# Forgetting attention and a GELU layer on one core: prefix sums on TensorE, w_in in smaller first pieces, an early first-layer product, v by SP's queue

## The chip, the cores and the metric

The kernel runs on one core of a Trainium2 chip. Its engines each follow their own instruction queue: TensorE (PE, with its weight loads PEld), VectorE (DVE), ScalarE (ACT), GpSimd (POOL) and SyncE (SP, which here only issues DMAs). The metric is the device time of one execution in microseconds; a kernel's time is the median of its runs. The time before is 332.49 us, the median of 3 runs (331.84 to 333.21).

## What is computed

Eight batches of eight heads, 576 positions, head size 64: causal attention in which each score gets the difference of two prefix sums of log f, followed by a two-layer MLP with a tanh GELU over the 4608 tokens (512 to 2048 to 512).

```python
scores = scale * np.matmul(q, k.transpose(0, 1, 3, 2))
log_f = np.log(np.clip(f, 0.0001, 1.0))
cum = np.cumsum(log_f, axis=-1)
decay = cum[:, :, :, None] - cum[:, :, None, :]
scores = np.where(causal, -1000000000.0, scores + decay)
attn = softmax(scores)                      # over the keys
x = np.matmul(attn, v)                      # heads side by side: 4608 x 512
h = x @ w_in
g = 0.5 * h * (1.0 + np.tanh(c * (h + 0.044715 * h * h * h)))
return g @ w_out
```

## The kernel before

**Quads.** Four heads of one batch are a quad; there are 16, two to a batch. A quad's queries and keys are loaded as bf16 (`LQ`, `LK`, by POOL's queue, which converts the type on the way) and transposed by DVE (`TQ`, `TK`, L209). The decay needs no work on the scores: the factor exp(-cum) of each key goes into the values (`vw`, on DVE, or `VW`, on POOL, L226) and into the weights of the denominators (`w_bf`); the query's factor cancels. So a quad is: scores on PE (`S`, or `H` for two of the four heads, L272), exp on ACT out of PSUM into `pt` (L280), causal masks on the diagonal blocks (`M` on POOL, L286; `m` as a multiply on DVE, L315), the denominators as a product on PE (`D`, followed on DVE by transpose, reciprocal, transpose), and two products with `vw` (`V`, x = 0 and 1) that DVE multiplies by the reciprocals into `xT` (L372). Quads 0 and 1, batch 0, are done in two parts of queries: part 0 is the first 256 positions, part 1 the other 320, and their scores come in four rounds, `split_rounds`. D.0.1 is quad 0, part 1; V.1.1.0 is quad 1, x = 1, part 0.

**The MLP.** Chunks of 512 tokens. Chunk 0's first layer is done in products of 256 tokens by 512 hidden columns: `J.half.g` (`mlp_in_half`, L404, 16 matmuls into a pair of PSUM banks of pool `psS`, then one GELU on ACT, L411). J.0.g needs part 0 of both quads in `xT`, J.1.g part 1. `F` and `f` are steps of the second layer (L597 for chunk 0, L530 later), f with 32-column weights; `I`, `E`, `U`, `UW`, `G`, `T` belong to the later chunks, whose products are saved by sums of blocks.

**The order is written out by hand.** `FRONT` is a string of words that are run one after the other; each engine gets its instructions in that order, and each queue its DMAs. A word `A@B` adds a wait: the first DMA of A starts only when B's has landed. `B.n.cols` issues n products of zeros of that many columns into `idle_ps`, a tile in the pool `psO` (one buffer, which `D` and `V` of the later quads use), so that PE has something to do. `X` and `Y` load ACT's table for exp and GELU.

**The prefix sums** (`SB` and `CW`). f is clipped by DVE, its logarithm taken by ACT, transposed on PE (L630) and copied to `logfT`, 5 tiles of 128 positions by 64 heads. POOL adds up the tiles before each tile (`before`, L648 and L650), and PE makes cum as a product with a triangle (L656, 320 columns) plus a product of ones with `before` (L657, 256 columns). ACT's exp of it is `wT`.

**Loads in the front.** POOL's queue has k and q of quads 0 and 1, then v of batch 0 row by row of 128 positions (`LP.t`), w_in in four pieces of 1024 hidden columns by half of the model dimension (`WI.c`, 8 KB of fp32 a partition), w_out in four (`WO.c`), v of batch 1 (`LX`: half of the heads, five DMAs), and the next quads' k and q. `Z` is five memsets on POOL. SP's queue carries f, and later v and the output. `LU.t` and `LV` are the same loads as `LP` and `LX` on SP's queue.

Of the kernel before, what the change touches and what calls it, by code (L numbers as in the profile page):

```python
# [8 lines left out]
FP32 = mybir.dt.float32  # L9
# [7 lines left out]
def kernel(  # L17
# [20 lines left out]
    D_MODEL, D_FF = moe_w_in.shape  # L38
# [20 lines left out]
    QA = 256  # L59
# [26 lines left out]

    SECOND = """
# [21 lines left out]
    singles = ctx.enter_context(tc.tile_pool(name="singles", bufs=1))  # L109
# [21 lines left out]
    vw = many(2, [128, NT + 1, 4, D], BF16, "vw")  # L131
# [4 lines left out]
    gT = singles.tile([128, N_FT, CH], BF16, name="gT")  # L136
# [13 lines left out]
    spare = singles.tile([1, 1], FP32, name="spare")  # L150
# [224 lines left out]
    def mlp_in(c, pr):  # L375

        n0 = CH * c % RING
        spans = [(n0, CH)] if n0 + CH <= RING else [(n0, HC), ((n0 + HC) % RING, HC)]
        ph = psS.tile([128, 2, 512], FP32, name="ps_h", tag="s")
        for dts in (range(N_DT - 1), range(N_DT - 1, N_DT)):  # L380
            for j in range(2):
                ft = 2 * pr + j
                for dt in dts:
                    for n, (h0, cols) in enumerate(spans):
                        nc.tensor.matmul(  # L385
                            ph[:, j, n * cols:(n + 1) * cols],
                            w_in_sb[:, dt, 128 * ft:128 * ft + 128],
                            xT[:, dt, h0:h0 + cols],
                            start=(dt == 0 and n == 0), stop=(dt == N_DT - 1),
                            skip_group_check=True,  # L390
                        )
                    if dt == N_DT - 1 and j == 1:
                        nc.scalar.activation(gelus(c, 2 * pr, 2), ph, AF.Gelu_apprx_tanh)  # L393
                    yield

    def mlp_in_half(half, g):

        ph = psS.tile([128, 2, 512], FP32, name="ps_h", tag="s")
        n0 = QA * half
        for dts in (range(N_DT - 1), range(N_DT - 1, N_DT)):  # L400
            for j in range(4):
                ft = 4 * g + j
                for dt in dts:
                    nc.tensor.matmul(  # L404
                        ph[:, j // 2, QA * (j % 2):QA * (j % 2) + QA],
                        w_in_sb[:, dt, 128 * ft:128 * ft + 128],
                        xT[:, dt, n0:n0 + QA],
                        start=(dt == 0 and j % 2 == 0), stop=(dt == N_DT - 1),
                        skip_group_check=True,
                    )  # L410
        nc.scalar.activation(gT[:, 4 * g:4 * g + 4, n0:n0 + QA],  # L411
                             ph.rearrange("p a (b n) -> p (a b) n", n=QA), AF.Gelu_apprx_tanh)

    def x_block(c, b, t):
        n0 = (CH * c + HC * t) % RING
        return xT[:, 2 * b:2 * b + 2, n0:n0 + HC]
# [227 lines left out]
            copy(m, utri_f32)  # L644
        copy(causal[1][64:128, 0:64], utri_f32[0:64, 0:64])

    def sums_before(eng):
        eng.tensor_copy(before[:, 0:BH], logfT[:, 0:BH])  # L648
        for t in range(1, NT - 1):
            eng.tensor_add(before[:, t * BH:(t + 1) * BH],  # L650
                                 before[:, (t - 1) * BH:t * BH],
                                 logfT[:, t * BH:(t + 1) * BH])

    def make_w():
        cum_ps = psM.tile([128, NT * BH], FP32, name="cum_ps", tag="m")
        nc.tensor.matmul(cum_ps, utri_f32, logfT, start=True, stop=False)  # L656
        nc.tensor.matmul(cum_ps[:, BH:], ones_f32, before, start=False, stop=True)  # L657
# [15 lines left out]
    def unit_part(c, u, n, spare=False):  # L673
        pull(units.setdefault((c, u), unit(c, u, spare)), n)
# [11 lines left out]
    def load_values(b, half):  # L686
# [104 lines left out]
```

## Time and profile before

| | us |
|---|---|
| median of 3 runs | 332.49 |
| the profiled execution | 332.24 |
| its span, first to last instruction | 330.4 |
| PE busy | 318.3 (96%) |
| DVE busy | 227.8 (69%) |
| ACT busy | 203.4 (62%) |
| POOL busy | 111.2 (34%) |

A busy PE counts idle products too, and a matmul at half clock as busy. The mean granted clock over the span is 0.990. Landmarks of the front, in us from the span's start: k and q of quad 0 land at 5.4 and 6.9; the cumulative sums end at 10.05; the first scores of quad 0 run at 10.69; the exps of quads 0 and 1 run from 11.49; D.0.1 ends at 26.05; the last product of chunk 0's first layer ends at 46.08; the second layer follows directly.

In a timeline row the first number is the start, the second the time to the end of the merged group, then engine, line, operation, output and input tiles, and the count; in square brackets stands the idle time before it and what ended it. In a row of waits: who waited for whom, total us, times, longest.

### The profile page before, as it was taken

The page shows a single profiled execution, that of the slowest core. Times are in us where ns is not written, and L with a number is a line of the kernel's source. Part 1 is how long each engine was busy: PE and PEld are TensorE (multiplying, and loading weights), DVE is VectorE, ACT ScalarE, POOL GpSimd, SP SyncE. Part 2 cuts the span into 40 slices and gives each one's busy share as a digit, 9 for nine tenths or more (in the row PEclk, how much of TensorE's full clock was granted, in tenths as well). Part 3 has the DMA queues.
Part 4 walks back from the last instruction along what each step waited for, and adds up shares of the span by engine and source line. Part 5 has one row for each costly group of instructions (what it writes and reads, how often), then busy time and mean ns, then how long its engine had stood idle before and what let it go on. Part 6 is the DMA issues. An engine that isn't in the chain of part 4 may idle for free.

```text
span 330.4 us, 12071 instructions
## 1 busy us (share of the span) xinstructions
PE 318.3 (96%) x5474; PEld 215.4 (65%) x5474; DVE 227.8 (69%) x360; ACT 203.4 (62%) x242; POOL 111.2 (34%) x155
## 2 busy tenths in 40 slices
PE   3988999999999999999999999999999999999996
PEld 1345864554677567765878877657765776587585
DVE  5574416985999967697777786779665865465373
ACT  4584476686766685587648765776668743712810
POOL 8985654152032506431444134412550140000000
PEclk9996999999999999999999999999999999999999
DMA  7999799576051991197118911661020102012002
GB/s 129 219 199 209 109 194 225 137 137 147 2 107 44 245 190 52 38 202 133 52 38 181 155 54 36 152 115 50 8 96 0 34 6 97 0 34 95 2 32 95
DMA packets 44322, 33.42 MB, mean 101 GB/s; under 512 B 27488, under 2 KB 37856, under 8 KB 44272
## 3 DMA queue, kind: packets, MB, share of 16 engines
q0 software_dynamic: 8848, 16.58, 28.2%
q1 hardware_dynamic: 35280, 16.01, 18.5%
q8 instruction: 42, 0.69, 0.8%
q10 hardware_dynamic: 144, 0.07, 0.1%
q14 instruction: 8, 0.07, 0.1%
HBM read 36.85 MB, written 9.44 MB: 140 GB/s over the span
## 4 chain that ended last, share of the span: by engine, by line
PE 92%; POOL 3%; DVE 2%; issue 1%; ACT 1%; POOLq 0%; DVEq 0%
PE ps_w L530 29%; PE ps_h L385 26%; PE ps_s L272 9%; PE po L340 9%; PE ps_u L451 6%; PE ps_h L404 5%; PE pso L597 4%; PE po_m L326 2%; PE idle_ps L251 1%; DVE pt L315 1%; ACT pt L280 1%; POOL v_nat L180 1%; POOL vw L226 1%; PE ps_o L340 0%; POOL q_c L203 0%
## 5 line engine op out<-in xcount | busy, mean ns | idle before, releaser
L280 ACT ACTIVATE pt<-ps_s 128x1024 bf16<-128x1024 f32 (+2 forms) x100 | 93.8, 988 | 48.0 <-PE ps_s L272 45.3
L385 PE MATMUL ps_h<-xT,w_in_sb 128*128 128x512 bf16 (+1 forms) x448 | 92.4, 356 | 0.0
L286 POOL TENSOR_SCALAR_AFFINE_SELECT pt<-pt 128x512 bf16<-128x512 bf16 (+3 forms) x65 | 39.6, 619 | 118.7 <-ACT pt L280 117.9
L385 PEld LDWEIGHTS <-w_in_sb 128*128 128x128 bf16 x448 | 43.8, 98 | 36.2 <-issue 0.4
L393 ACT ACTIVATE gT<-ps_h 128x1024 bf16<-128x1024 f32 x44 | 44.7, 1017 | 22.6 <-PE ps_h L385 22.2
L530 PEld LDWEIGHTS <-gT 128*32 128x32 bf16 (+1 forms) x1354 | 45.0, 97 | 3.8 <-issue 0.4
L530 PE MATMUL ps_w<-w_out_sb,gT 128*32 128x256 bf16 (+1 forms) x954 | 41.3, 273 | 0.0
L530 PEld LDWEIGHTS <-gsum 128*32 128x32 bf16 (+1 forms) x984 | 35.3, 97 | 3.4 <-issue 1.5
L272 PE MATMUL ps_s<-qT,kT 32*128 32x64 bf16 (+5 forms) x896 | 37.1, 266 | 0.1
L226 POOL TENSOR_TENSOR vw<-v_nat,wT 128x1280 bf16<-128x1280 f32 (+1 forms) x13 | 29.5, 2267 | 10.4 <-DMA v_nat<-in_v_dram 6.9
L209 DVE STREAM_TRANSPOSE kT<-k_c 128x576 f32<-128x576 f32 x16 | 19.9, 1246 | 12.2 <-DMA k_c<-in_k_dram 12.2
L272 PEld LDWEIGHTS <-kT 32*128 32x128 bf16 x896 | 17.1, 93 | 17.1 <-issue 12.0
L530 PE MATMUL ps_w<-usum,gsum 128*32 128x256 bf16 (+1 forms) x779 | 28.3, 273 | 0.0
L547 DVE COPY snap<-ps_w 128x512 f32<-128x512 f32 x32 | 21.6, 676 | 7.8 <-PE ps_w L530 7.8
L372 DVE TENSOR_TENSOR xT<-po,rb 128x576 bf16<-128x576 f32 x26 | 19.6, 756 | 9.9 <-PE po L340 9.2
L340 PE MATMUL po<-pt,vw 128*32 128x64 bf16 (+4 forms) x624 | 22.5, 279 | 0.0
L508 DVE TENSOR_TENSOR gsum<-gT 128x1024 bf16<-128x1024 bf16 x14 | 9.7, 692 | 18.3 <-ACT gT L464 13.1
L467 DVE TENSOR_TENSOR usnap<-ps_u,usnap 128x512 f32<-128x512 f32 x21 | 13.8, 683 | 12.3 <-PE ps_u L451 7.9
L340 PEld LDWEIGHTS <-vw 128*32 128x32 bf16 x672 | 14.4, 97 | 10.5 <-issue 3.7
L209 DVE STREAM_TRANSPOSE qT<-q_c 128x576 f32<-128x576 f32 x16 | 19.9, 1243 | 1.3 <-PE ps_s L272 0.7
L464 ACT ACTIVATE gT<-usnap 128x512 bf16<-128x512 f32 x18 | 11.1, 630 | 9.5 <-DVE usnap L467 9.5
L530 PE MATMUL ps_w<-w_out_sb,gsum 128*128 128x256 bf16 (+2 forms) x205 | 16.6, 269 | 0.0
(109 smaller groups left out, 414.5 us busy)
## 6 DMA issues: line engine op xcount, KB each, us to landing
out_dram<-o_st SPq DMA_DIRECT2D x35, 256.0 KB, 2.3
k_c<-in_k_dram POOLq DMA_DIRECT2D x16, 288.0 KB, 5.7
q_c<-in_q_dram POOLq DMA_DIRECT2D x16, 288.0 KB, 6.2
v_nat<-in_v_dram SPq DMA_DIRECT2D x16, 256.0 KB, 4.7
w_in_sb<-in_moe_w_in_dram POOLq DMA_DIRECT2D x4, 512.0 KB, 9.7
w_out_sb<-in_moe_w_out_dram POOLq DMA_DIRECT2D x4, 512.0 KB, 7.1
v_nat<-in_v_dram SPq DMA_DIRECT2D x16, 128.0 KB, 3.8
v_nat<-in_v_dram POOLq DMA_DIRECT2D x13, 128.0 KB, 7.5
```

The costliest lines, as they stand in the source:

```text
L209: nc.vector.transpose(out=dst.rearrange("p s c -> p (s c)").bitcast(FP32) .rearrange("p (t a) -> p a t", a=S // 32), in_=src.rearrange("p ...
L226: eng.tensor_mul(vw[i % 2][:, t0:t1], vb[:, t0:t1, h0:h0 + 4, :], wT[:, i, t0:t1, :].unsqueeze(3).to_broadcast([128, t1 - t0, 4, D]))
L272: nc.tensor.matmul(tiles[h // 2][:, h % 2, c0:c0 + nq], key_columns(i, key, h, c), qq[32 * h:32 * h + 32, q0:q0 + nq, c], start=(c == 0 an ...
L280: nc.scalar.activation(p[:, 2 * g:2 * g + 2, off:off + n], t[:, :, 0:n], AF.Exp, scale=scale)
L286: nc.gpsimd.affine_select(out=x, in_=x, compare_op=ALU.is_ge, fill=0.0, base=0, pattern=pattern, channel_multiplier=-1)
L340: nc.tensor.matmul(po[r0:r0 + w.shape[-1], 448 + q0:448 + q0 + nq], w, p[:, h, col:col + nq], start=(key in (0, "low")), stop=(key in ("lo ...
L372: nc.vector.tensor_mul(xT[:, 2 * u + x, r0 + s0:r0 + s1], po, rbs[i, part])
L385: nc.tensor.matmul(ph[:, j, n * cols:(n + 1) * cols], w_in_sb[:, dt, 128 * ft:128 * ft + 128], xT[:, dt, h0:h0 + cols], start=(dt == 0 and ...
L393: nc.scalar.activation(gelus(c, 2 * pr, 2), ph, AF.Gelu_apprx_tanh)
L451: nc.tensor.matmul(ps[:, n, :], w[:, d, 128 * n:128 * n + 128], x[:, d, :], start=(first and n == 0 and d == 0), stop=(d == 1), skip_group ...
L530: nc.tensor.matmul(ps[c0:c0 + width, n, cols[0]:cols[1]], x[:, j, 128 * n + c0:128 * n + c0 + width], w[:, j, cols[0]:cols[1]], start=(fir ...
L547: copy(kept[name], ps)
```

## The change

The prefix sums move from POOL to PE; w_in's first 1024 hidden columns come in pieces of 512; one product of the first layer, J.0.0, is made early as `j.0.0` in the bank pair that the idle products used, and its GELU is issued later, as `GJ.0.0`; part of batch 0's v and the halves of later batches that POOL's queue brought go by SP's queue; and the words of `FRONT` stand in a new order. No `B` follows `j.0.0` any more. After the cut the rest of the order up to the end of `FRONT` holds the same work with small moves (F.1's steps are 97 in both).

```diff
     SETUP = """
-        TK.0 LP.4 LP.0 LP.1
+        TK.0 LP.0 LP.1
     """
     FRONT = """
-        TQ.0 SB TR B.1.512 TK.1 LP.2@LQ.0 CW B.1.256 B.1.512 WI.0 S.0.0 B.5.384 TQ.1 S.0.2 LQ.2 B.2.512 Z H.1.0.1 vw.0.0 B.2.128 vw.1.0 M.0.0 LP.3
-        B.1.128 WI.1@LU.4 H.1.1.1 B.3.384 W WI.3 WI.2 H.1.0.0 M.1.0.1 D.0.0 M.1.0.0 H.0.1.1 V.0.0.0 H.0.1.0 B.3.128 H.1.1.0 M.0.1 V.0.1.0 D.1.0 H.0.3.0
-        vw.0.1 LX.1.1 V.1.0.0 H.0.3.1 m.0.3.2 V.1.1.0 H.1.3.0 B.1.256 m.0.3.4 VW.1.1 H.1.3.1 D.0.1 M.1.3 S.1.2 M.1.1 V.0.0.1 LK.2 V.0.1.1 WO.0 J.0.1
-        D.1.1 WO.1@LV.1.1 J.0.0 V.1.1.1 V.1.0.1 VW.3 J.0.3 J.1.3 WO.2@WI.1 J.1.1 WO.3 J.1.0 LK.3 LQ.3 TQ.2 J.0.2 LQ.4 TK.2 LX.1.0@WO.2 J.1.2 X B.1.128
-        f.0.6 LK.4 TK.3 S.2.0 LK.5 f.0.5 F.0.4 S.2.2 F.0.10 S.2.1 TQ.3 TQ.4 F.0.10 m.2.1 LV.2.0@LK.5 vw.2 S.3.0 TK.4 CL.2 M.2.2 f.0.7 LQ.5 M.2.0 D.2
+        Z CW TR TQ.0 B.1.512 WI.1 WI.0 LU.3@LU.1 S.0.0 B.5.384 LU.2@LU.0 TQ.1 TK.1 S.0.2 LU.4@LU.1 B.2.512 H.1.0.1 vw.0.0 M.0.0 vw.1.0 B.2.128 B.1.384
+        WI.3 WI.2 B.1.256 H.1.1.1 B.1.256 W H.1.0.0 M.1.0.1 B.1.512 LQ.2 D.0.0 M.1.0.0 H.0.1.1 WI.4 V.0.0.0 B.2.128 H.0.1.0 M.0.1 V.0.1.0 LV.1.1@WI.3
+        H.1.1.0 WI.5 D.1.0 H.0.3.0 B.2.128 V.1.0.0 H.0.3.1 m.0.3.2 V.1.1.0 H.1.3.0 vw.0.1 j.0.0 H.1.3.1 m.0.3.4 M.1.3 D.0.1 S.1.2 M.1.1 VW.1.1 V.0.0.1
+        LK.2 V.0.1.1 WO.0 GJ.0.0 D.1.1 V.1.1.1 J.0.1 WO.1@LV.1.1 V.1.0.1 J.1.1 WO.2 J.0.2 TQ.2 WO.3 J.1.0 J.0.3 TK.2 LQ.3 LK.3 VW.3 J.1.2 LQ.4 J.1.3
+        LV.1.0@WO.2 X F.0.1 LK.4 TK.3 F.0.4 F.0.1 S.2.0 f.0.8 f.0.3 S.2.2 F.0.10 S.2.1 TQ.3 TQ.4 LK.5 F.0.10 LV.2.0@LK.5 m.2.1 S.3.0 vw.2 CL.2 M.2.2
...
     def load_w_in(c):
-        n, u = D_FF // 2, c % 2
-        s = slice(n * (c // 2), n * (c // 2 + 1))
+        u, n = c % 2, D_FF // 4
+        s = (slice(0, n), slice(n, 2 * n), slice(2 * n, 4 * n))[c // 2]
...
+    later = {}
+
-    def mlp_in_half(half, g):
+    def mlp_in_half(half, g, spare=False):
 
-        ph = psS.tile([128, 2, 512], FP32, name="ps_h", tag="s")
+        if spare:
+            ph = psO.tile([128, 1024], FP32, name="ps_h", tag="po").rearrange("p (a n) -> p a n", n=512)
+        else:
+            ph = psS.tile([128, 2, 512], FP32, name="ps_h", tag="s")
...
-        nc.scalar.activation(gT[:, 4 * g:4 * g + 4, n0:n0 + QA],
+        later[half, g] = lambda: nc.scalar.activation(gT[:, 4 * g:4 * g + 4, n0:n0 + QA],
                              ph.rearrange("p a (b n) -> p (a b) n", n=QA), AF.Gelu_apprx_tanh)
+        if not spare:
+            later[half, g]()
...
-    def sums_before(eng):
-        eng.tensor_copy(before[:, 0:BH], logfT[:, 0:BH])
-        for t in range(1, NT - 1):
-            eng.tensor_add(before[:, t * BH:(t + 1) * BH],
-                                 before[:, (t - 1) * BH:t * BH],
-                                 logfT[:, t * BH:(t + 1) * BH])
-
     def make_w():
         cum_ps = psM.tile([128, NT * BH], FP32, name="cum_ps", tag="m")
-        nc.tensor.matmul(cum_ps, utri_f32, logfT, start=True, stop=False)
-        nc.tensor.matmul(cum_ps[:, BH:], ones_f32, before, start=False, stop=True)
+        nc.tensor.matmul(cum_ps, utri_f32, logfT, start=True, stop=True)
+        for n in range(NT - 1, 0, -1):
+            nc.tensor.matmul(cum_ps[:, n * BH:], ones_f32, logfT[:, :(NT - n) * BH], start=False, stop=True,
+                             skip_group_check=True)
...
+        "j": lambda half, g: mlp_in_half(half, g, True),
+        "GJ": lambda half, g: later[half, g](),
```

At the end of `FRONT` the load of batch 3's second half of v, `LX.3.1@LK.6`, becomes `LV.3.1@LK.6`.

More of the change, by code (lines that the diff above doesn't have):

```diff
@@ L79 @@
-        D.1.1 WO.1@LV.1.1 J.0.0 V.1.1.1 V.1.0.1 VW.3 J.0.3 J.1.3 WO.2@WI.1 J.1.1 WO.3 J.1.0 LK.3 LQ.3 TQ.2 J.0.2 LQ.4 TK.2 LX.1.0@WO.2 J.1.2 X B.1.128
-        f.0.6 LK.4 TK.3 S.2.0 LK.5 f.0.5 F.0.4 S.2.2 F.0.10 S.2.1 TQ.3 TQ.4 F.0.10 m.2.1 LV.2.0@LK.5 vw.2 S.3.0 TK.4 CL.2 M.2.2 f.0.7 LQ.5 M.2.0 D.2
-        S.3.1 f.0.7 m.3.0 V.2.0 S.3.2 f.0.6 TK.5 f.0.1 M.3.2 CL.3 V.2.1 S.4.1 m.3.1 LQ.6 F.0.6 TQ.5 H.4.2.1 D.3 LQ.7 H.4.0.1 VW.4 H.4.0.0 V.3.1 v.3.0
-        f.0.2 H.4.2.0 LV.2.1@LQ.5 LK.6 I.1.1 U.0 m.4.1 I.1.4 I.1.6 I.1.0 TQ.6 U.1 m.4.2.3 I.1.5 m.4.2.2 CL.4 LV.3.0@LQ.7 M.4.0 TK.6 G.0 I.1.2 U.3 I.1.3
@@ L83 @@
-        U.2 I.1.7 G.1.1.2 X UW.2.1 UW.2.2 F.1.20 UW.2.3 VW.5 S.5.0 F.1.19 S.5.1 D.4 M.5.0 f.1.12 S.5.2 V.4.0 f.1.9 m.5.2.3 V.4.1 CL.5 m.5.2.2 LQ.8
-        UW.2.4 S.6.0 M.5.1 f.1.12 D.5 S.6.1 f.1.7 LK.7 V.5.1 f.1.7 vw.6 S.6.2 V.5.0 f.1.11 m.6.1 M.6.2.2 m.6.0 m.6.2.3 LK.8 CL.6 LX.3.1@LK.6
+        Z CW TR TQ.0 B.1.512 WI.1 WI.0 LU.3@LU.1 S.0.0 B.5.384 LU.2@LU.0 TQ.1 TK.1 S.0.2 LU.4@LU.1 B.2.512 H.1.0.1 vw.0.0 M.0.0 vw.1.0 B.2.128 B.1.384
+        WI.3 WI.2 B.1.256 H.1.1.1 B.1.256 W H.1.0.0 M.1.0.1 B.1.512 LQ.2 D.0.0 M.1.0.0 H.0.1.1 WI.4 V.0.0.0 B.2.128 H.0.1.0 M.0.1 V.0.1.0 LV.1.1@WI.3
@@ new lines @@
+        H.1.1.0 WI.5 D.1.0 H.0.3.0 B.2.128 V.1.0.0 H.0.3.1 m.0.3.2 V.1.1.0 H.1.3.0 vw.0.1 j.0.0 H.1.3.1 m.0.3.4 M.1.3 D.0.1 S.1.2 M.1.1 VW.1.1 V.0.0.1
+        LK.2 V.0.1.1 WO.0 GJ.0.0 D.1.1 V.1.1.1 J.0.1 WO.1@LV.1.1 V.1.0.1 J.1.1 WO.2 J.0.2 TQ.2 WO.3 J.1.0 J.0.3 TK.2 LQ.3 LK.3 VW.3 J.1.2 LQ.4 J.1.3
+        LV.1.0@WO.2 X F.0.1 LK.4 TK.3 F.0.4 F.0.1 S.2.0 f.0.8 f.0.3 S.2.2 F.0.10 S.2.1 TQ.3 TQ.4 LK.5 F.0.10 LV.2.0@LK.5 m.2.1 S.3.0 vw.2 CL.2 M.2.2
+        f.0.7 M.2.0 D.2 S.3.1 LQ.5 f.0.6 V.2.0 m.3.0 TK.4 S.3.2 f.0.1 CL.3 LK.6 TK.5 f.0.3 f.0.2 M.3.2 V.2.1 S.4.1 m.3.1 LQ.6 F.0.6 TQ.5 H.4.2.1 D.3
@@ L85 @@
+        H.4.0.1 H.4.0.0 VW.4 V.3.1 v.3.0 f.0.2 H.4.2.0 I.1.1 LV.2.1@LQ.5 LQ.7 U.0 m.4.1 I.1.4 I.1.6 TQ.6 m.4.2.3 I.1.0 I.1.5 m.4.2.2 CL.4 LV.3.0@LQ.7
+        U.1 TK.6 M.4.0 G.0 U.2 I.1.2 UW.2.1 U.3 I.1.3 I.1.7 G.1.1.2 F.1.20 UW.2.2 X S.5.0 UW.2.3 VW.5 F.1.19 S.5.1 D.4 M.5.0 f.1.12 S.5.2 V.4.0 f.1.10
+        UW.2.4 m.5.2.3 m.5.2.2 V.4.1 CL.5 LQ.8 M.5.1 S.6.0 f.1.13 D.5 S.6.1 f.1.5 V.5.1 f.1.9 LK.7 vw.6 S.6.2 V.5.0 m.6.1 M.6.2.2 m.6.0 F.1.2
+        LV.3.1@LK.6 m.6.2.3 F.1.7 CL.6 LK.8
     """
@@ L144 @@
     logfT = singles.tile([128, NT * BH], FP32, name="logfT")
-    before = singles.tile([128, (NT - 1) * BH], FP32, name="before")
     wT = singles.tile([128, NQ, NT, 4], FP32, name="wT")
@@ L692 @@
         "CW": make_w,
-        "SB": lambda: sums_before(nc.gpsimd),
-        "sb": lambda: sums_before(nc.vector),
         "Z": zeros,
```

## The prediction

> **What bounds the kernel now.** I read the slices of the span first, then the waits of PE, then the first 47 us window by window, then each engine's timeline there. In the page's slices PE is full but for the first and for one dent, and in the fourth slice (24.8 to 33.0 us) the granted clock falls to 0.6.
>
> ```profile
> PE   3988999999999999999999999999999999999996
> PEclk9996999999999999999999999999999999999999
> ```
>
> So PE bounds everything, and time can only come from the front. What PE waited for up to 80 us, and the windows of 1 us around the dent (sum, then PE, PEld, DVE, ACT, POOL busy, then clock, DMA share, GB/s):
>
> ```profile
> PE po_m L326 <- DVE pt L315: 2.3, 2, 1.5
> PE cum_ps L657 <- POOL before L650: 1.1, 1, 1.1
> ```
>
> ```profile
> 22.00:23.00 1.00, 0.98 (x19) 0.58 (x18) 1.00 (x3) 1.00 (x3) 1.00 (x3) 1.00 1.04 182
> 23.00:24.00 1.00, 0.24 (x12) 0.07 (x7) 1.00 (x2) 0.66 (x1) 1.00 (x2) 1.00 1.17 213
> 24.00:25.00 1.00, 0.31 (x8) 0.10 (x8) 1.00 (x2) 0.00 (x0) 1.00 (x2) 0.67 1.08 203
> 25.00:26.00 1.00, 0.17 (x8) 0.10 (x8) 0.78 (x1) 0.00 (x0) 1.00 (x2) 0.50 1.11 215
> 31.00:32.00 1.00, 1.00 (x15) 0.65 (x17) 0.00 (x0) 0.11 (x1) 0.59 (x1) 0.92 1.20 192
> ```
>
> The denominators of quad 0's second part (D.0.1) wait for two masks on DVE (m.0.3.2, m.0.3.4); behind them PE is idle for most of 22.8 to 26.05 us, and the clock is at half from 24.34 us (0.67 in that window) to 31.16 us (0.92). That costs twice: the stage after the wait is slow too, as the chain of waits shows, where 16 matmuls of the first layer take 3.00 us and later 96 take 10.59 us, 1.77 for 16:
>
> ```profile
> 28.85 3.00 PE ps_h L404 x16
> ...
> 35.49 10.59 PE ps_h L404 x96
> ```
>
> Of the slow 6.82 us PE worked in 26.05 to 31.16, so half of 5.11, 2.55 us, is lost to the clock. Why the masks are late stands in the timelines of DVE and POOL: the first takes 1.36 us while POOL issues five loads of v, the second 1.65 us while POOL makes vw; the same mask with POOL idle takes 0.42 us (56.23).
>
> ```profile
> 20.47 3.65 POOL L180 DMA_DIRECT2D v_nat<-in_v_dram  x5
> 24.11 1.51 POOL L226 TENSOR_TENSOR vw<-v_nat,wT 128x768 bf16<-128x768 f32 x1
> ...
> 22.51 1.36 DVE L315 TENSOR_TENSOR pt<-pt,causal 128x512 bf16<-128x512 bf16 x1
> 24.13 1.65 DVE L315 TENSOR_TENSOR pt<-pt,causal 128x256 bf16<-128x256 bf16 x1
> 56.23 0.42 DVE L315 TENSOR_TENSOR pt<-pt,causal 128x512 bf16<-128x512 bf16 x1
> ```
>
> Ahead of it, from 11.5 to 23.7 us, ACT's exps run almost without a gap (pitch 0.65, 0.73 and 0.9 us for 640, 768 and 1024 columns), and each score product on PE waits for the exp two before it.
>
> **The change, step by step.** I follow PE through the new order; "before" is the same event in the trace.
>
> Prefix sums. POOL's copy and three additions (7.26 to 8.79) go, and PE's wait of 1.07 us. In place of one 256-column product there are four, 64 to 256 columns, 640 in all. The trace has two such shapes:
>
> ```profile
> 6.35 1.41 PE L656 MATMUL cum_ps<-logfT,utri_f 128*128 128x320 f32 x2
> ...
> 8.83 1.22 PE L657 MATMUL cum_ps<-before,ones_f 128*128 128x256 f32 x2 [1.07 <-POOL before L650]
> ```
>
> The difference of 0.19 us for 64 columns, 3.0 ns a column, is the low bound: 1.9 us; with each product's fixed 0.45 us (1.22 less 256 x 3.0 ns) it is 3.7 us. I take 2.9, the middle, since weight loads (0.25 us each) overlap partly. From 7.7 that ends at 10.6 (9.6 to 11.4), before 10.05. Of the idle products behind it 256 columns are gone (0.64 us before, about 0.3 now), so S.0.0 starts at 10.95 instead of 10.69 and its exps at 11.8 instead of 11.49.
>
> DVE's new order (causal copies ahead of TQ.0, TQ.1 ahead of TK.1): qT is ready at 8.8, before S.0.0; kT of quad 1 is ready at 13.96 (q lands at 11.44, two transposes of 1.26), before 11.16, and H.1.0.1 starts only at 14.9, when an exp frees its bank. Cost nothing; without that cover it would be 2.8.
>
> Exps and idle products up to H.1.3.0. S.0.2's exps start at 14.15 (13.85). H.1.0.1 is now followed by 128, 128, 384 and 256 idle columns (0.58 us by rows of 0.09, 0.20 and 0.20) instead of three of 128 (0.27), and 256 and 512 columns stand where 3 x 384 (0.59) stood; another 256 follow V.0.0.0 and 256 D.1.0. With scores of 0.5 to 0.6 and products of 0.3 us PE is now as long as ACT's pitch: H.1.1.1's exp starts at 16.7 (16.00), H.0.1.1's at 18.6 (17.87), H.0.3.1's at 22.4 (21.40), H.1.3.0 ends on PE at 23.15 (22.02). So the front arrives 1.1 us later here (0.3 to 1.9 by the bounds above).
>
> The early product j.0.0, 16 matmuls, 1.77 us, goes here, 23.15 to 24.95. It needs w_in's first 512 columns, issued at about 8.1 and 8.8 behind POOL's memsets (1.7 us, moved up); the 1024-column piece issued at 9.62 landed 7.8 us later, so they are there by 17 to 18. It needs xT from V.1.1.0 for its last four: with the loads of v off POOL's queue the mask m.0.3.2 starts with its exp at 23.15 and takes 0.42, then V.1.1.0's multiply 0.41, to 24.0; the last four start at 24.5. Then vw.0.1 (0.92, moved behind) to 24.9 and m.0.3.4, 0.27, to 25.2. SP now brings v's rows 2, 3 and 4, issued when rows 0 and 1 have landed (14.35 before); SP's loads of v took 4.2 us, so they are there by 20. Only other loads of v stand behind that wait in SP's queue. H.1.3.1 runs 24.95 to 25.5 and its exp ends at 26.25 (23.67). D.0.1 starts at 25.5 with its masks done, so the wait of 2.3 us is gone and PE has no gap from which the clock would fall.
>
> One rule speaks against the mask's 0.42 us. The Trainium skill, SBUF — State Buffer, "Who interferes with whom", has a vector instruction with two SBUF inputs block against a GpSimd instruction that reads SBUF, and infers that it does not against the writing of DMA descriptors. The 1.65 us beside vw agrees (it ends 0.16 us behind it); the 1.36 us beside mere DMA issues does not. By the rule m.0.3.2 would stay at 1.36 and the sum below come out 0.6 us smaller.
>
> What is late next. POOL had made vw for V.1.1.1 by 25.6; now it masks first: 1.70 us for M.1.3 and M.1.1, then 1.51 for VW.1.1, all behind H.1.3.1's exp, to 29.5. PE meanwhile: D.0.1 to 26.15, S.1.2 to 26.65 (its second bank is free at 26.3), V.0.0.1 and V.0.1.1 1.15, D.1.1 from 28.0 (S.1.2's exps) to 28.65; then V.1.1.1 waits 0.9 to 29.55. V.1.1.1 0.58, J.0.1 1.77, V.1.0.1 0.58, two matmuls of J.1.1, then a wait of 0.4 for V.1.0.1's multiply (0.49), since nothing stands between: J.1.1 ends at 34.65. The remaining five J at 1.77 end at 43.5. GJ.0.0 and the table load (1.28 and 1.02) lie on ACT at 28 to 30.5, under these products. Before, the last J ends at 46.08 and 0.06 of idle product follows: **2.6 us** earlier.
>
> The loads. Q of quad 2 is issued behind half of w_in, k behind VW.1.1 at 29.5 (27.2); w_out's four go at 30.1 to 32.4, before 27.8, 31.4, 37.9 and 38.7 (landed 45.5), since they no longer stand behind VW.3. By 1888 KB of such loads landed in 12.5 us from 37.93, 151 KB a us, quad 2's k and w_out, 2336 KB, need 15.5 us: 45.0, or 47.9 if quad 3's q and k and v's half (another 1152 KB) interleave, at the 190 KB a us of those windows. F.0's twelfth step, which first needs the last piece, comes at 47.1 (six steps of 0.235, S.2.0 0.7, six more). I take nothing; up to 0.8 if not.
>
> Behind 46 us PE is full in every window up to 262, the work is the same, and order and queues (v by SP for batches 1 and 3, k and q some places later) only move cover. I take nothing, with 0.5 either way.
>
> **Sum.** 330.4 - 2.6 = 327.8 of span; the execution was 332.24 and the median 332.49, so 329.6 for that execution and 329.9 for the median.
>
> **Rivals.**
> (1) The masks stay slow beside POOL: 2.0 us gained, 330.5. For it the rule above; against it that POOL issues nothing between WI.5 (about 21) and M.1.3 (26.3).
> (2) Loads are late: w_out (0.8) and with it quad 3's transposes take back 1.6 us: 331.5. For it the DMA share of 1.0 from 2 to 37 us; against it the pause at 38 to 40 (0.01), which goes, and SP's cheaper bytes (8.9% of the engines for 1.88 MB against 80.9% for 10.97).
> (3) The front's shift eats the gain: the prefix sums take 3.7 us, 0.8 more, and the idle products and the scores behind them slip by as much again: j.0.0 starts at 24.75 and 1.0 remains: 331.5. For it the exps' pitch, which leaves PE no slack from 16 us on; against it that ACT waits too, so that a slip before 16 us is partly made good.
> (4) Slower: the wait moves to V.1.1.1 and takes the clock along. POOL's 3.2 us chain hangs on H.1.3.1's exp, which j.0.0 pushes back 2.6. The clock fell about 1.4 us after PE's steady work ended (22.95 to 24.34), so from a wait of 1.4 instead of 0.9 it falls again, and the work of the next seven us runs at half: 0.5 + 3.3 lost, 333.7. For it: nothing in that chain is spare, each of POOL's four instructions there follows on the one before. Against it: PE works right up to that wait. The Trainium skill, TensorE: Matmul & The Clock Gate, Part 1, has the clock decided in free-running windows of about 3.4 us; by that a wait of 1.4 alone would not do it, though before the 3.2 us of idling here fit.
>
> **Numbers.** Forecast 0.58, (1) 0.10, (2) 0.10, (3) 0.10, (4) 0.12. Half a per cent (1.66 us) is about what a measurement of this kernel tells from no change: faster is below 330.83, the forecast but for a tenth and most of (1), some of the rest: 0.65; slower, above 334.15, only the worse half of (4) and the unforeseen: 0.09; the rest 0.26. The forecast's own range is 328.3 to 331.2 (prefix sums and idle products 0.8, tail 0.5); with (2) and (3), each with 1.3 for the same unknowns, it reaches 332.8, and (4) with 0.12 is left out.
>
> **What would show it.** Right: granted clock 1.0 from 10 to 46 us; L315's masks under 0.5 us; j.0.0 without a gap, ending near 25; the last J near 43.5; a new wait of about 0.9 on POOL's vw. Wrong: a second dent in the clock near 29 to 36, waits on w_in or w_out, or cumulative sums ending past 11.4.

## The result and the profile after

The changed kernel took 328.17 us in the median of 20 runs (326.76 to 334.38), the kernel before beside it 332.26 (330.57 to 333.71). The ratio is 0.9867, with a 95% interval of 0.9848 to 0.9887: faster by about 4.4 us, where 2.6 were forecast. Thirteen of the 20 executions lie between 326.8 and 329.0; seven took 331.9 to 334.4, and the comparison leaves those out. They have a cause of their own, shown below: the profile that was taken of the changed kernel is one of them (334.38), so the usual execution is read from a second profile of the very same kernel (run a_again, 327.39, span 325.7 against 330.4 before).

The slices of its page, PE's busy share and the granted clock:

```profile
PE   3998999999999999999999999999999999999996
PEclk9999999999999999999999999999999999999999
```

The dent of the fourth slice is gone, in PE as in the clock. What PE waited for up to 80 us, behind the prefix sums, and three of the windows round the old dent (sum, then PE, PEld, DVE, ACT, POOL busy, then clock, DMA share, GB/s):

```profile
PE po_m L326 <- POOL vw L226: 0.4, 1, 0.4
PE ps_s L272 <- ACT pt L280: 0.4, 1, 0.4
PE ps_h L409 <- DVE xT L372: 0.3, 1, 0.3
```

```profile
22.00:23.00 1.00, 1.00 (x12) 0.87 (x9) 1.00 (x3) 0.32 (x1) 0.00 (x0) 1.00 1.15 201
...
24.00:25.00 1.00, 0.98 (x28) 0.33 (x20) 0.59 (x2) 0.58 (x2) 0.39 (x1) 1.00 1.04 144
25.00:26.00 1.00, 1.00 (x40) 0.82 (x41) 0.86 (x3) 1.00 (x2) 1.00 (x3) 1.00 1.03 158
```

The wait of 2.3 us is gone and with it the seven us at half clock. What is left are three waits of 0.3 to 0.4, for vw at 27.7 us, for an exp in S.0.2 at 12.5 and for xT at 31.2, and the clock stays at 1.00. PE's timeline has j.0.0, H.1.3.1 and D.0.1 without a wait, and DVE's the two masks:

```profile
21.32 1.92 PE L409 MATMUL ps_h<-xT,w_in_sb 128*128 128x256 bf16 x16
23.17 0.52 PE L272 MATMUL ps_s<-qT,kT 32*128 32x320 bf16 x8
23.62 0.70 PE L326 MATMUL po_m<-pt,w_bf 128*32 128x320 bf16 x20
```

```profile
21.61 0.42 DVE L315 TENSOR_TENSOR pt<-pt,causal 128x512 bf16<-128x512 bf16 x1 [0.59 <-ACT pt L280]
...
23.15 0.28 DVE L315 TENSOR_TENSOR pt<-pt,causal 128x256 bf16<-128x256 bf16 x1
```

So far this is what was forecast. The rest of the gain, nearly 2 us, appears in PE's timeline of the first microseconds. First the kernel before, then a_again:

```profile
10.63 0.82 PE L272 MATMUL ps_s<-qT,kT 32*128 32x256 bf16 x16
11.38 1.78 PE L251 MATMUL idle_ps<-idle 128*128 128x384 bf16 x5
13.10 0.72 PE L272 MATMUL ps_s<-qT,kT 32*128 32x320 bf16 x8
```

```profile
7.48 2.55 PE L658 MATMUL cum_ps<-logfT,ones_f 128*128 128x64 f32 x8
9.83 0.63 PE L251 MATMUL idle_ps<-idle 128*128 128x512 bf16 x1
10.40 0.52 PE L272 MATMUL ps_s<-qT,kT 32*128 32x256 bf16 x16
10.85 0.99 PE L251 MATMUL idle_ps<-idle 128*128 128x384 bf16 x5
11.81 0.32 PE L272 MATMUL ps_s<-qT,kT 32*128 32x320 bf16 x2
```

The same five idle products take 1.78 us before and 0.99 after, the same 16 score products 0.82 and 0.52. The array was at about half speed there in the kernel before, though the page's clock row has 9 in those slices and the windows 1.00. The clock record in the trace explains it: its first entry, full speed, stands at 14.10 us in the kernel before and at 10.36 in a_again, and the page counts the time ahead of the first entry as full speed. S.0.2's first scores run at 11.81 instead of 13.10.

| event, us | before | forecast | a_again |
|---|---|---|---|
| S.0.0 starts | 10.69 | 10.95 | 10.46 |
| S.0.2's exps start | 13.85 | 14.15 | 12.89 |
| H.1.1.1's exp starts | 16.00 | 16.7 | 15.25 |
| H.1.3.0 ends on PE | 22.02 | 23.15 | 21.38 |
| j.0.0 ends | | 24.95 | 23.24 |
| D.0.1 ends | 26.05 | 26.15 | 24.32 |
| wait of V.1.1.1 for vw | | 0.9 | 0.40 |
| last J ends | 46.08 | 43.5 | 41.65 |

The last J ends 4.4 us earlier, and the execution is 4.85 shorter than the profiled one before: nothing of it is given back behind the last J.

**The long executions.** In the first profile of the changed kernel the front is as in a_again up to 28 us. Then POOL's timeline has, and PE's waits answer it:

```profile
28.34 0.76 POOL L196 DMA_DIRECT2D w_out_sb<-in_moe_w_out_dram  x1
38.23 2.23 POOL L196 DMA_DIRECT2D w_out_sb<-in_moe_w_out_dram  x3 [9.13 <-DMA v_nat<-in_v_dram]
```

```profile
PE pso L604 <- DMA w_out_sb<-in_moe_w_out_dram: 5.3, 3, 3.0
```

`WO.1@LV.1.1` holds POOL until SP has brought the second part of v for batch 1. Those five loads of SP took 9.6 to 14.7 us to land, with a median of 11.5, and SP was held up in issuing them too, as the chain of waits shows (start, us, what):

```profile
22.25 5.76 SPq L180
28.06 9.64 DMA v_nat<-in_v_dram
```

So the last three loads of w_out go out at 38.23. From 35 to 39 us the DMA engines are nearly idle (share 0.07 in that window): POOL waits, and nothing else has been issued. The second layer's first products (L604) then wait for w_out, three times, and the clock is at 0.50 from 52 to 55 us. In a_again POOL's wait for v is 3.14 us, the loads go out at 32.12, and PE does not wait for w_out up to 80 us. Why SP's loads land later in some executions than in others, no run here shows.

```profile
32.12 2.23 POOL L196 DMA_DIRECT2D w_out_sb<-in_moe_w_out_dram  x3 [3.14 <-DMA v_nat<-in_v_dram]
```

### The profile page after: what moved, and what is told of

It is laid out like the page before. It is cut to its first block, busy times and chain, and to the rows that moved or that the text cites. A ratio compares the mean times of both kernels' runs of the same rounds, so it can differ in the third digit from the quotient of the medians.

```text
span 332.7 us, 11990 instructions
## 1 busy us (share of the span) xinstructions
PE 315.8 (95%) x5426; PEld 215.8 (65%) x5444; DVE 225.6 (68%) x360; ACT 203.6 (61%) x242; POOL 97.7 (29%) x135
## 4 chain that ended last, share of the span: by engine, by line
PE 82%; DMA 8%; POOL 3%; SPq 2%; issue 2%; DVE 1%; ACT 1%; POOLq 0%; DVEq 0%
PE ps_w L537 28%; PE ps_h L385 26%; PE po L340 8%; PE ps_s L272 8%; PE ps_u L458 6%; PE pso L604 4%; DMA w_out_sb<-in_moe_w_out_dram 3%; DMA v_nat<-in_v_dram 3%; SPq L180 2%; DMA w_in_sb<-in_moe_w_in_dram 2%; ACT pt L280 1%; POOL pt L286 1%; PE cum_ps L658 1%; POOL vw L226 1%; DVE vw L226 0%
## 5 line engine op out<-in xcount | busy, mean ns | idle before, releaser
L604 PE MATMUL pso<-w_out_sb,gT 128*32 128x512 bf16 (+1 forms) x157 | 16.4, 388 | 5.8 <-DMA w_out_sb<-in_moe_w_out_dram 5.3
L203 POOL DMA_DIRECT2D k_c<-in_k_dram x16 | 9.1, 566 | 37.8 <-DVE kT L209 28.2
```

The costliest lines, as they stand in the source:

```text
L604: nc.tensor.matmul(pso[c0:c0 + cols, :], gT[:, ft, 128 * n + c0:128 * n + c0 + cols], w_out_sb[:, ft, :], start=(ft == 0), stop=(ft == N_F ...
```

## The experiments

All were timed in five rounds beside the kernel before; its medians in the three sets were 333.01, 333.03 and 332.0. "The base" is the changed kernel without the gate on w_out (a_nogate), and of a changed line of `FRONT` only the words around the change are shown.

**a_again: the changed kernel once more.**

> The changed kernel once more, for a profile beside its kin. Theory (late loads): most executions near 328 us; in them the second layer's first steps hardly wait for w_out, and in the longer ones, near 332 to 334, they wait 5 us or more, because w_out's second piece waits on POOL's queue for v of batch 1 from SP's queue. Rival (the clock): the longer executions have the same waits as the shorter ones and only a lower clock.

327.85 us (326.99 to 327.95), ratio 0.9841 [0.9817, 0.9866]. All five are of the usual kind. What it shows is above: the gain over the forecast is already there at 21.3 us.

**a_nogate: w_out not held for v.**

```diff
-V.1.1.1 J.0.1 WO.1@LV.1.1 V.1.0.1
+V.1.1.1 J.0.1 WO.1 V.1.0.1
```

> The changed kernel without the wait of w_out's second piece for v of batch 1 (WO.1 for WO.1@LV.1.1). Theory (late loads): w_out's four pieces are issued in one go near 28 to 31 us, no execution is above 330 us any more, the median comes to 326 to 328. Rival (the clock): a third of the executions still stand 4 to 6 us above the others. Second rival (the wait is needed): v of batch 1 comes later by 3 us or more, VW.3 and quad 3 with it, and the time is 329 or more.

327.24 us (326.74 to 327.35), ratio 0.9828 [0.9804, 0.9852]. POOL's timeline:

```profile
28.49 2.99 POOL L196 DMA_DIRECT2D w_out_sb<-in_moe_w_out_dram  x4
```

The four loads go out in one row, and no DMA is waited for by PE up to 80 us. Of 40 executions of the versions without the gate that are told of here (n_big_w_in apart), one lies above 330 us (330.49); with it, seven of 25. So the gate makes the long executions; in the usual one it costs nothing that these runs can tell (0.9841 with it, 0.9828 without).

**a_no_early and n_no_early: the early product undone**, first in the changed kernel, then in the base.

```diff
-H.1.3.0 vw.0.1 j.0.0 H.1.3.1
+H.1.3.0 vw.0.1 B.1.256 H.1.3.1
...
-WO.0 GJ.0.0 D.1.1 V.1.1.1 J.0.1 WO.1 V.1.0.1 J.1.1
+WO.0 D.1.1 V.1.1.1 J.0.1 WO.1 V.1.0.1 J.0.0 J.1.1
```

> The changed kernel with the early product undone: J.0.0 in its own bank pair ahead of J.1.1, and one idle product of 256 columns in its old place. Theory (the early product covers the wait for the masks): PE idles 1.5 us or more there or D.0.1 follows at once because the masks are quick; if it idles the clock falls as before and the time is 3 us above the changed kernel's. Rival (the masks were the cost, not the missing cover): with v off POOL's queue the masks take 0.4 and 0.3 us, D.0.1 starts 1.4 to 1.9 us sooner, the clock stays, and the time is within 1 us of the changed kernel's.

331.42 us over all (328.18 to 334.92), ratio 0.9899 [0.9865, 0.9934]. Three of its eight executions are above 334; in the profile, which is of one of them, the gate holds POOL for 11.4 us and PE waits for w_out as well as at D.0.1. So the same edit without the gate:

> The base without w_out's wait, and with the early product undone (J.0.0 ahead of J.1.1, one idle product in its place). Theory (the early product covers the wait for the masks): D.0.1 waits 1.0 to 1.4 us, the granted clock halves for 2 to 3 us, and the time is 1.5 to 2.5 us above the base's 327.2. Rival (the 8 executions with this edit and the wait were long because of late loads alone): within 0.5 us of the base.

328.97 us (328.47 to 329.94), ratio 0.9905 [0.988, 0.993], against 327.24 and 0.9828 for the base, which ran in another set: 1.7 us by the medians, 2.6 by the ratios (0.0077 of 332.5). PE's timeline at D.0.1, the mask that it waits for in DVE's, and the windows:

```profile
23.56 0.22 PE L326 MATMUL po_m<-pt,w_bf 128*1 128x64 bf16 x4 [1.21 <-DVE pt L315]
```

```profile
22.78 0.72 DVE L315 TENSOR_TENSOR pt<-pt,causal 128x256 bf16<-128x256 bf16 x1
```

```profile
22.00:23.00 1.00, 0.35 (x12) 0.14 (x5) 1.00 (x2) 0.63 (x1) 0.29 (x1) 1.00 1.08 198
23.00:24.00 1.00, 0.44 (x12) 0.22 (x11) 0.68 (x2) 0.00 (x0) 1.00 (x3) 0.59 1.03 145
24.00:25.00 1.00, 1.00 (x20) 0.42 (x16) 0.93 (x3) 0.53 (x1) 1.00 (x2) 0.50 1.03 166
...
26.00:27.00 1.00, 1.00 (x36) 0.68 (x29) 0.48 (x2) 1.00 (x1) 1.00 (x2) 0.71 1.14 207
```

Prefix sums, queues and the order of the masks are the new ones, yet the second mask, which stands behind vw.0.1 on DVE and takes 0.72 beside POOL's own masks, is late by 1.21 us for D.0.1, and the clock falls, from about 23.2 to 26.6. The early product is no extra work: it is the cover of that wait, and it keeps the clock. That is the forecast's main step, shown.

**b_early: the early product alone in the kernel before**, with the smaller pieces of w_in that it needs.

```diff
-V.1.1.0 H.1.3.0 B.1.256 m.0.3.4
+V.1.1.0 H.1.3.0 j.0.0 m.0.3.4
...
-WO.0 J.0.1 D.1.1 WO.1@LV.1.1 J.0.0 V.1.1.1
+WO.0 GJ.0.0 J.0.1 D.1.1 WO.1@LV.1.1 V.1.1.1
```

> The kernel before with two parts of the change alone: w_in's first 1024 columns in 512-column pieces and the early product in the place of one idle product, its GELU after w_out's first piece. Sums, loads of v and order stay as before. Theory (cover and clock are most of the gain): the clock stays at full, D.0.1 still waits up to 1.5 us for the slow masks beside POOL, and 2.5 to 4 us of the 4 to 5 come. Rival (without v off POOL's queue the cover is too small): the wait stays above 1.4 us, the clock falls again, and 1 to 2 us come.

329.17 us (328.5 to 332.19), ratio 0.9921 [0.9887, 0.9956]: 2.6 us, with 1.5 to 3.8 possible. DVE's masks and PE's j.0.0, in the profile of its longest execution:

```profile
22.54 1.36 DVE L315 TENSOR_TENSOR pt<-pt,causal 128x512 bf16<-128x512 bf16 x1
...
24.16 0.28 DVE L315 TENSOR_TENSOR pt<-pt,causal 128x256 bf16<-128x256 bf16 x1
```

```profile
22.68 1.25 PE L409 MATMUL ps_h<-xT,w_in_sb 128*128 128x256 bf16 x10 [0.29 <-DVE xT L372]
24.29 0.60 PE L409 MATMUL ps_h<-xT,w_in_sb 128*128 128x256 bf16 x4 [0.36 <-DVE xT L372]
```

The first mask is as slow as before, so `xT` comes late and j.0.0 waits twice, 0.65 us in all; but nothing waits at D.0.1, and the clock is 1.00 in every window from 22 to 34. So this one step brings 2.6 of about 4.4 us even with a slow mask; a quick first mask would be worth the two short waits at most. That the profiled execution (332.19) is no shorter than the kernel before has its cause far behind this: the second layer starts 3.9 us sooner (42.18 and 46.06), PE's last product still ends 1.6 us sooner (325.48 and 327.11), and SP takes 2.42 us instead of 0.84 to issue the last two stores.

**b_fill: the kernel before with PE kept busy between its two prefix products.** It asks whether the gap of 1.07 us there is what held the array at half speed.

```diff
+        keep_busy(3)
         nc.tensor.matmul(cum_ps[:, BH:], ones_f32, before, start=False, stop=True)
```

> The kernel before with three idle products of 512 columns between the two products of the prefix sums, where PE waits 1.07 us for POOL. Theory (the array's clock rises only after some us of unbroken work, and the wait puts this off): the idle products of 384 columns behind S.0.0 take 0.2 us each instead of 0.32, S.0.2's exps start 0.4 to 0.8 us sooner, and the time falls by 0.3 to 0.8 us. Rival (those products are slow for another reason, or ACT sets the pace): the exps of S.0.2 start as before, and the time is the same or up to 0.4 us longer.

331.77 us (330.58 to 333.77), ratio 0.9974 [0.9953, 0.9995]: 0.9 us, with 0.2 to 1.6 possible. PE's timeline and its waits:

```profile
7.36 1.44 PE L251 MATMUL idle_ps<-idle 128*128 128x512 bf16 x3
8.63 0.68 PE L658 MATMUL cum_ps<-before,ones_f 128*128 128x256 f32 x2
...
10.02 0.99 PE L251 MATMUL idle_ps<-idle 128*128 128x384 bf16 x5
10.99 0.32 PE L272 MATMUL ps_s<-qT,kT 32*128 32x320 bf16 x2
```

```profile
PE po_m L326 <- DVE pt L315: 2.3, 2, 1.5
PE po_m L326 <- DVE w_bf L684: 0.8, 1, 0.8
```

Three products of zeros make the array fast: 0.68 us where 1.22 stood, 0.99 where 1.78 stood. The first entry of the clock record moves from 14.10 to 8.61 us. So the fast start that the forecast had not seen also comes with products of zeros: it needs PE at work, not this work. Half of what is won is lost again to a new wait of 0.8 for `w_bf`: H.1.0.0 starts 1.79 us sooner than in the kernel before (14.69 and 16.48), D.0.0 behind the wait 0.90 (16.03 and 16.93); the mask waits stay.

**n_pool_sums: the base with the sums back on POOL** (`before` and its product as in the kernel before, `SB` ahead of `Z`).

```diff
-Z CW TR TQ.0 B.1.512
+SB Z CW TR TQ.0 B.1.512
```

> The changed kernel without the wait of w_out's second piece (its base here), and with the prefix sums back on POOL (a copy and three additions, ahead of the memsets) and one product of ones behind them. Theory (the four products keep PE at work, and the array's clock rises early): PE waits about 1 us for POOL, the five idle products of 384 columns take 0.3 us each, S.0.2's exps start 0.5 to 0.9 us later than in the base, and the time is 0.5 to 1.2 us longer. Rival (the four products are simply dearer than one, as forecast): the front arrives 0.3 to 0.9 us sooner and the time is that much shorter.

327.08 us (326.58 to 330.49), ratio 0.9844 [0.9801, 0.9888]: no difference from the base. PE's timeline:

```profile
8.09 1.22 PE L665 MATMUL cum_ps<-before,ones_f 128*128 128x256 f32 x2 [0.33 <-POOL before L658]
...
9.67 0.83 PE L273 MATMUL ps_s<-qT,kT 32*128 32x256 bf16 x16
10.43 1.78 PE L252 MATMUL idle_ps<-idle 128*128 128x384 bf16 x5
```

The sums are ready 0.7 us sooner than with four products, because POOL works on them 0.7 us sooner than in the kernel before (6.58 and 7.26) and PE waits 0.33 instead of 1.07. The array is slow until 12.14, as it was in the base's profile (12.04), so the short gap need not be what kept it slow. S.0.2's exps start at 12.64, not later than in the base (13.16) as the theory had it, and j.0.0 0.5 us sooner (21.08 and 21.59); the times do not tell the two apart. The part of the change that its title names first, prefix sums on TensorE, brings nothing that these runs can tell.

**n_v_pool: the base with v of batch 1 on POOL's queue again.**

```diff
-M.0.1 V.0.1.0 LV.1.1@WI.3
+M.0.1 V.0.1.0 LX.1.1
```

> The base without that wait, and with batch 1's second half of v by POOL's queue again (LX.1.1, at the place where LV.1.1 stood). Theory (POOL's issuing of loads slows the masks on DVE): five issues of 0.73 us run on POOL from about 20 to 24 us, the first mask on DVE takes over 1 us instead of 0.42, M.1.3 starts where it did or up to 0.5 us later, and the time is 0.3 to 1.5 us longer. Rival (the mask has cover): j.0.0 hides the slow mask, and the time is the same within 0.3 us.

327.32 us (327.01 to 328.2), ratio 0.9838 [0.9806, 0.9871]: no difference. POOL's and DVE's timelines:

```profile
20.37 3.66 POOL L180 DMA_DIRECT2D v_nat<-in_v_dram  x5
```

```profile
21.86 0.42 DVE L315 TENSOR_TENSOR pt<-pt,causal 128x512 bf16<-128x512 bf16 x1 [0.60 <-ACT pt L280]
...
23.40 0.28 DVE L315 TENSOR_TENSOR pt<-pt,causal 128x256 bf16<-128x256 bf16 x1
```

This takes away a reason of the forecast: the same five loads are issued right beside both masks, and the masks are quick. So the masks can be quick without v's move to SP.

**n_big_w_in: the base with w_in in four pieces of 1024 columns**, `WI.4` and `WI.5` taken out of the order.

```diff
-        s = (slice(0, n), slice(n, 2 * n), slice(2 * n, 4 * n))[c // 2]
+        s = slice(n * (c // 2), n * (c // 2 + 1))
```

> The base without that wait, and with w_in in four pieces of 1024 columns (the first two where the 512-column pieces were, the others where the second two were). Theory (the small pieces only matter for j.0.0): the first two pieces, twice as large, land at 18 to 21 us, j.0.0 starts at 21.4 as before or waits under 0.5 us, and the time is the same within 0.5 us. Rival (the loads of v behind them are pushed back): v's rows 2 to 4 land 3 us later, vw.0.1 and D.0.1 wait for them, and the time is 1 us longer or more.

334.54 us (333.38 to 337.64), ratio 1.006 [1.0033, 1.0087]: 7 us more than the base, slower than the kernel before. DVE's timeline, PE's waits, and the landing times of SP's loads issued from 10 to 40 us:

```profile
28.89 0.96 DVE L226 TENSOR_TENSOR vw<-v_nat,wT 128x768 bf16<-128x768 f32 x1 [6.69 <-DMA v_nat<-in_v_dram]
```

```profile
PE po_m L326 <- DVE pt L315: 7.3, 1, 7.3
```

```profile
v_nat<-in_v_dram SPq DMA_DIRECT2D x2, 256.0 KB, 14.2
```

It is not j.0.0 that comes late (21.16 us), but v of batch 0: SP's two loads of 256 KB take 14.2 us to land (4.3 in a_again) while POOL's queue has the bigger pieces outstanding. vw.0.1, now ahead of the mask on DVE, holds the mask, the mask holds D.0.1 for 7.3 us, and the clock falls.

**n_big_v_pool: the same big pieces, but v of batch 0 by POOL's queue and ahead of w_in.**

```diff
-Z CW TR TQ.0 B.1.512 WI.1 WI.0 LU.3@LU.1 S.0.0 B.5.384 LU.2@LU.0 TQ.1 TK.1 S.0.2 LU.4@LU.1
+Z CW TR TQ.0 B.1.512 LP.3 LP.2 LP.4 WI.1 WI.0 S.0.0 B.5.384 TQ.1 TK.1 S.0.2
```

> The kernel with w_in in 1024-column pieces (334.5) and v's rows 2 to 4 by POOL's queue, ahead of w_in, as before the change. Theory (SP's loads are starved while POOL's queue holds large loads, and v's rows were what was missing): the rows land by 20 us, vw.0.1 does not wait, and the time is 326.8 to 328.3. Rival (the size of the pieces itself costs): 331 or more, with j.0.0 or J.0.1 waiting for w_in.

328.03 us (327.33 to 328.69), ratio 0.9875 [0.9849, 0.9901]. Nearly all of the 7 us comes back, so the size of the pieces does not cost it by itself: what does is v of batch 0 behind them on SP's queue. Queue and place were changed together here, so which of the two counts is not told apart. With small pieces v can go by SP (4.3 us in a_again).

**n_swap and n_best: other work in front of the two new waits.** V.1.1.1 waits for POOL's vw, J.1.1 for V.1.0.1's multiply; other words can stand there.

```diff
-D.1.1 V.1.1.1 J.0.1 WO.1 V.1.0.1 J.1.1 WO.2 J.0.2
+D.1.1 J.0.1 WO.1 V.1.1.1 V.1.0.1 J.0.2 WO.2 J.1.1
```

> The base without that wait, and with J.0.1 moved ahead of V.1.1.1 and J.0.2 between V.1.0.1 and J.1.1. Theory (the two waits of 0.4 and 0.3 us there are on the path): both vanish, the last J ends 0.6 to 0.7 us sooner, and the time falls by 0.4 to 0.8 us to about 326.6. Rival (something behind sets the pace, w_out or the transposes of quad 3): the J end sooner, a wait of the same size appears behind 41 us, and the time is the same within 0.3 us.

326.87 us (326.21 to 327.66), ratio 0.9822 [0.9789, 0.9855]: against the base 0.4 us by the medians, which the intervals do not separate. Both waits are gone, but J.0.2 now waits 0.54 for w_in, whose later half is not there yet. n_best leaves J.0.2 in its place and puts only J.0.1 ahead and V.1.0.1 before V.1.1.1:

```diff
-D.1.1 V.1.1.1 J.0.1 WO.1 V.1.0.1 J.1.1
+D.1.1 J.0.1 WO.1 V.1.0.1 V.1.1.1 J.1.1
```

> The base without w_out's wait, with J.0.1 ahead of V.1.0.1 and V.1.1.1, and these two exchanged, so that J.1.1's third matmul needs the earlier one. Theory (the waits of 0.4 and 0.3 us there are on the path): both vanish and no wait on w_in takes their place, the time falls by 0.5 to 0.8 us to 326.4 to 326.8. Rival (w_out or quad 3 sets the pace behind): the same within 0.3 us.

326.68 us (325.86 to 327.51), ratio 0.9835 [0.9807, 0.9863]. PE's timeline:

```profile
26.28 0.70 PE L326 MATMUL po_m<-pt,w_bf 128*32 128x320 bf16 x20 [0.31 <-DVE xT L372]
26.91 1.92 PE L409 MATMUL ps_h<-xT,w_in_sb 128*128 128x256 bf16 x16
28.77 1.22 PE L326 MATMUL po_m<-pt,vw 128*32 128x320 bf16 x40
29.92 10.65 PE L409 MATMUL ps_h<-xT,w_in_sb 128*128 128x256 bf16 x96
```

Behind the first of these rows none has a wait, and the last J ends at 40.57. It is faster than the kernel before by 1.65%. Against the changed kernel it is 1.2 us lower by the medians (327.85 in a_again), against the base 0.6; by the ratios (0.9841, 0.9828) there is nothing between them, so the forecast gain of 0.5 to 0.8 is neither shown nor excluded. None of its five executions is a long one.

## Why the prediction was right in its mechanism and short in its size

**The dent.** Right. The wait at D.0.1 and the half clock behind it went, and n_no_early and b_early show from both sides that the early product is what does it: without it 1.7 to 2.6 us are lost, alone it brings 2.6.

**The term that was mis-sized** is "So the front arrives 1.1 us later here", at the end of the step on the exps and idle products up to H.1.3.0. It arrived 0.6 us sooner (21.38 against 22.02), 1.8 from the forecast, outside the bounds of 0.3 to 1.9 later. That is nearly the whole of the 1.85 us by which the last J came earlier than forecast. The table has it in three parts.

- 0.5 is there at S.0.0: the four prefix products took 2.55 us, not 2.9, and began 0.2 sooner.
- 0.8 more comes up to S.0.2's exps, 2.43 us behind S.0.0 instead of 3.20, with the scores and the five idle products at full speed (0.99 instead of 1.78). The step priced the work before 14 us at the durations of the kernel before, as if a row had one price, while its other rows (0.09 and 0.20) were those of the fast array. The page's clock row hid the difference; the two durations of one shape, 1.78 / 5 = 0.36 there and 0.22 from 15.88 us on, were in the trace to be seen.
- The last 0.5 gathers up to H.1.3.0. The step counted the 256 idle columns behind V.0.0.0 and the 256 at D.1.0, but not that three products of 128 columns behind H.0.1.0 (0.34 us, at 18.60 before) are gone: from H.1.1.1's exp on it charged 0.43 us more than before, and a_again took 0.11 more.

b_fill shows what put full speed off in the kernel before: without the break in PE's work it came at 8.61 us, with it at 14.10 (b_early, which has the break too, 14.64). These are single profiles, and where exactly it comes is in part luck: with the same PE instructions in this stretch as a_again it came at 9.52 in n_no_early and at 12.04 in a_nogate, whose five idle products took 1.42 us. That spread of 2.5 us is less than half of what b_fill moved. And the front was early whenever it came: in the profiles with the new front j.0.0 started between 21.1 and 21.7 us, 1.5 to 2.1 sooner than forecast.

**The masks.** The forecast of 0.42 and 0.27 was right, its reason is not borne out. It laid the 1.36 us on POOL's issuing of v; n_v_pool has the issuing and 0.42. In the kernel before, in b_early and in b_fill the mask began 0.5 us into the third issue and ended 0.39 to 0.41 us behind the start of the fifth (23.87 and 23.46 in the kernel before); in n_v_pool it began with the third issue (21.86 and 21.88). That would fit a block that depends on which of the two starts first, but n_v_pool's second mask began 0.05 us behind the start of the fifth issue (23.40 and 23.35) and took 0.28, and no run varied the moment alone, so it stays open. The Trainium skill, SBUF — State Buffer, "Who interferes with whom", says that issue order decides who blocks; the rows at 24 us do not settle it: POOL's vw started 0.02 us ahead of the second mask in the kernel before, where the mask took 1.65, and 0.01 us ahead in b_early, where it took 0.28. Its inference that such an instruction does not collide with descriptor writing fits n_v_pool and not the other three.

**What is late next.** V.1.1.1 waited 0.40, not 0.9, J.1.1 0.28 for 0.4, and S.0.2 waited 0.39 for an exp at 12.52, which had not been counted. The waits stood where they were expected, the first at less than half its size, and the clock stayed at 1.00.

**The rivals.** (1), slow masks, did not come; b_early shows what it would have cost, two waits of 0.65 us together. (3), the prefix sums, went the other way. (4), the clock falling at V.1.1.1, did not come at 0.40 us. Its threshold, a wait of 1.4, is not borne out: in n_no_early the clock fell 0.8 us after PE's steady work ended (22.35 to 23.2), in a wait of 1.21 between spells of part work, while in the long execution of the changed kernel a wait of 1.33 for w_out, up to 43.96, left it at 1.00. What decides stays open. The Trainium skill, TensorE: Matmul & The Clock Gate, Part 1, has the clock fall after an idle window of about 3.4 us; in n_no_early PE was busy 0.35 and 0.44 of 22 to 24 us, so that trace does not agree, while the 3.4 us at half that followed do have the length of its window.

(2), loads late, is what happens in a third of the changed kernel's executions (7 of 20), at 331.9 to 334.4, no faster than the kernel before, by a path close to the one named: not by the bytes but by `WO.1@LV.1.1`, which hung on SP's loads. The forecast let w_out's four go at 30.1 to 32.4, which needs SP's five loads, issued from about 20 us on, there by 30; those of 128 KB took 10.2 to 11.1 us to land in a_again and 11.5 to 14.7 in the long execution. For v of batch 0 its 4.2 us was right (4.3).

**The tail.** "I take nothing" behind 46 us held, with the 0.5 either way that it allows: 4.4 us at the last J, 4.85 in the execution.

## What to carry to other kernels

Take the price of a filler or warm-up instruction from rows of its own stretch of the trace, and compare the durations of one shape over time: they tell the array's speed even where the clock row has nothing to say. A dent that costs twice, by the wait and by the clock, is best covered by work that is needed anyway and ready early, even if the wait's own cause stays. A load that gates others should not hang on a second queue whose landing times swing (SP's loads of 128 KB here: 9 to 17.5 us).

## What the runs showed of the hardware that was not expected

- The granted clock of the page is 1.00 from the start, while the same idle product of 384 columns took 0.36 us on average (1.78 for five) before the clock record's first entry and 0.20 (0.99 for five) behind it. Full speed came 3.8 us (b_fill, from 4.79 to 8.61), 4.1 us (a_again, from 6.28 to 10.36) and 5.3 us (the kernel before, from 8.83 to 14.10) after the start of unbroken work, and with a_again's PE instructions also after 3.2 us (n_no_early) and 5.8 us (a_nogate).
- The stretches at half clock before the end lasted 3.41 us (n_no_early, b_fill, the long execution), 6.83 us (the kernel before) and 10.24 us (n_big_w_in), by the clock records: once, twice and three times the same length.
- SP's loads of v of 256 KB landed after 4.3 us (a_again) or 14.2 us (n_big_w_in), those of 128 KB issued from 19 us on after 9.0 (a_nogate) to 17.5 us (a_no_early), and the issue of one of them took 5.76 us.
- One mask on DVE took 0.42 or 1.36 us beside the same five loads issued by POOL.
